# Two transformer layers on one core: another order of the opening, two key spans at the layer boundary, and exchanged places for the opening's partial sums

## The chip, the core and the metric

The kernel runs on one core of a Trainium2 chip. The core has TensorE (PE, matrix multiply), VectorE (DVE), ScalarE (ACT), GpSimd (POOL) and SyncE (SP), which issues the DMAs. Each engine takes its own instructions in the order in which the program lists them, and waits where one needs the result of another engine. The metric is the device time of one execution in microseconds.

## The reference, cut to what matters

Two layers, each of attention and a feed-forward block, over S = 2048 rows of D = 448 columns, with 16 heads of 28 columns. Both layers use the same weights.

```python
def _A_ref(x, wqkv, wo):
    qkv = (x @ wqkv).reshape(B, S, 3, H, Dh).transpose(2, 0, 3, 1, 4)
    q, k, v = qkv[0], qkv[1], qkv[2]
    p = softmax(einsum("bhqd,bhkd->bhqk", q, k) * Dh ** -0.5)
    return einsum("bhqk,bhkd->bhqd", p, v).transpose(0, 2, 1, 3).reshape(B, S, D) @ wo
def _B_ref(x, w1, b1, w2, b2):
    h = maximum(x @ w1 + b1, 0)
    return (h * h) @ w2 + b2
for _ in range(2):
    x = x + _A_ref(layernorm(x), wqkv, wo)
    x = x + _B_ref(layernorm(x), w1, b1, w2, b2)
```

The hidden width F is 1792. Inputs and outputs are bf16. Softmax needs 16 heads x 2048 x 2048 exponentials in each layer.

## The kernel before, in words

**Scores and exponentials.** Heads are taken four at a time (a group g of four; G = 4 groups), each head in 32 rows of its own, so that four small matmuls run side by side. A *unit* is one head's scores of 256 queries against 256 keys (or 128 queries against 512 keys): 512 columns of 128 partitions, one PSUM bank. There are 2048 units, 1024 in each layer. Up to three units make one score group in a PSUM tile `sc` (line 809), and one exponential on ScalarE (line 834) turns them into bf16 weights `pt`. Two such tiles are in turn.

VectorE takes some of the third units of a group off ScalarE and computes their exponential with five operations (lines 890, 904, 910, 916 and 923): the first reads the scores from PSUM, the others build the power of two and a polynomial. Its scratch is `v_i`, `v_e`, and where possible a second set in a part of the K tile of the other layer that is not in use. `apart` decides which unit goes there: none in the last `STOP` units; none when the load of VectorE over the past 14 us is above `BUSY`, or above `LOW` if the feed-forward work is behind a line that `LINES` draws (first unit, last unit, number of blocks); and when fewer than `LAG` units are left in the current pass, it takes one of the next pass, whose keys must be there.

**Passes.** A *pass* is one query block, one group g and one span of keys. Its products with V (line 983) add up in one PSUM bank. When a pass does not cover all keys, its sum is copied aside by VectorE (line 1006), and later passes of the same block and group add to it (line 1008). `part` names the place of such a partial sum: it lies in the K tile of the other layer, 256 columns of float32 for each block, from the end of the tile backwards. In layer 0 that tile's last 512 bf16 columns are also VectorE's second scratch set, for query blocks 2 to 6.

The order of the passes is a list. In layer 0 `OPENING` gives (block, first key tile, last key tile) for query blocks 0 and 1, since keys come in while scores already run; the other blocks take all 16 key tiles at once. At the boundary, query blocks 0 to 2 of layer 1 start on the keys that are already made while the last blocks of layer 0 still pass through projection and feed-forward: `CUTS` splits the key tiles into spans, and within a span all three blocks and four groups come in turn (lines 662 to 664). The unit numbers follow: layer 1 starts at unit 1024; a span of n key tiles for three blocks and four groups takes 24 n units.

**The rest of a layer.** `first_block` normalises two tiles of 128 rows, transposes them (line 493, evicted on line 505), and `qkv` makes K (evicted on lines 573 and 575), Q (569 and 571) and V (601 and 603). `early` blocks (the first two) may use ScalarE for evictions, up to score group 8, and the banks of the score tiles. `chain` does the rest for a query block: output projection with the sum to x (line 1114), layer norm (line 448), hidden layer (1161 and 1168), second product, and in layer 0 the Q, K and V of layer 1.

**What sets the order.** Each of these is a stream of operations with a priority (a small number goes first) and an estimated duration. A planner picks, step by step, the operation that can start first, and writes the instructions in that order; it holds lower work on TensorE back if it would make the next scores late. So a change of a priority or a threshold moves instructions everywhere after it. Priorities: scores 0, exponentials 1, products with V 2, VectorE's first step 1.5, evictions 3.5, `chain` 4 and up, a VectorE unit's other steps `V_PRIO`, and 3.6 (`V_LATE`) once `V_WAIT` us have passed, and 1.8 once the unit is `V_AGE` groups old or its pass is `V_PAST` units past.

Of the kernel before, what the change touches and what calls it, by code (L numbers as in the profile page):

```python
# [18 lines left out]
G = 4  # L19
QB = 512  # L20
QR = 256
# [14 lines left out]
DCLK = 0.2  # L36
OWN = 2
HALF = 320
LINES = ((280, 1312, 8.0), (1440, 2040, 7.0))
MARGIN = 2.0  # L40
LOW = 0.6
TURNS = 1
ENDU = 100
HOTE = 0.8
WSTOP = ('wk', 0)
XT = 1
VEND = 1
OPENING = ((0, 0, 2), (0, 2, 4), (1, 0, 4), (0, 4, 8), (1, 4, 8), (0, 8, 12), (0, 12, 16), (1, 8, 16))
ONE = 1
GATE = [None, None, ('Q', 0, 0, 0), ('Q', 0, 0, 0), ('s', 8), ('s', 8), ('s', 8), ('s', 8)]  # L50
EARLY = 2
# [1 line left out]
SLACK = 0.5  # L53
WINDOW = 2.8
C_PRIO = 1.5
V_PRIO = 6.0
V_LATE = 3.6
V_LAST = 1.8
V_AGE = 7
V_PAST = 2  # L60
OWN3 = 0
FIRST = 90
V_FIRST = 9.2
V_WAIT = 4.5
NEAR = 9
FAR = 15
KEEP = 4
LAG = 6
LEAD = 20
LAST = 690  # L70
BUSY = 0.95
SPAN = 14.0
NPT = 11
NOS = 3
# [11 lines left out]
THIRD = 1  # L86
NL = 0
NLP = 3.8
STOP = 90
HSTOP = 0  # L90
CHUNK = 2
EV = 3.5
CUTS = (0, 8, 12, 16)


class Res:
# [121 lines left out]
def kernel(  # L218
# [13 lines left out]
    _, S, D = A_x.shape  # L232
# [28 lines left out]
    pl = Planner()  # L261
# [13 lines left out]
    wv = const.tile([P, NDC, D], DT.bfloat16, name="wv")  # L275
# [12 lines left out]

    def part(l, qb, g):
        keys = K_sb[1 - l][:, g, :].bitcast(DT.float32)  # L290
        return keys[:, S // 2 - (qb + 1) * QR:S // 2 - qb * QR]

    st_qk = V_sb[1][:, :, :, :].rearrange("p t h r -> p (t h r)")[:, 0:NDC * 2 * D]
    st_qk = st_qk.rearrange("p (c n) -> p c n", c=NDC)
# [240 lines left out]
    def mm_tile(subs, evac, ev_dur, deps, any_engine=False, sets=(), early=False, post=(), acq=None, alone=0):  # L535


        box = {}
        mms = [(c0, n, lhsT, rhs, i == 0, i == len(ops) - 1, own)
               for c0, n, ops in subs for i, (lhsT, rhs, *own) in enumerate(ops)]  # L540
        first = last = None
        i = 0
        while i < len(mms):
            dur, k = 0.003, i
            while k < len(mms) and (k == i or dur + mms[k][1] / 2400 < (0.6 if i == 0 and alone else 0.46) and not (alone and k == alone)):
                dur += max(0.07, mms[k][1] / 2400 + 0.003)
                k += 1

            def fn(e, part=mms[i:k], i=i):
                if i == 0:  # L550
                    box["t"] = bank(first, "mt")
                for c0, n, lhsT, rhs, a, b, _ in part:
                    nc.tensor.matmul(box["t"][:, c0:c0 + n], lhsT=lhsT() if callable(lhsT) else lhsT, rhs=rhs,  # L553
                                     start=a, stop=b)
            own = list({d for m in mms[i:k] for d in m[6]})
            last = Op("PE", dur, fn, deps=(list(deps) if i == 0 else [last]) + own,
                      acq=None if i else pools_now(early) if early else spare(len(mms)))
            first = first or last
            yield last
            i = k  # L560
        e = Op(engs_now(early) if any_engine else ("DVE",), ev_dur, lambda e: evac(e, box["t"]), deps=[last], rel=first, acq=acq, sets=sets)
        pl.spawn(EV, iter([e, *[p(e) for p in post]]))
        return e
# [14 lines left out]
    def qkv(l, t0, nt, xnT, own_xt, ends, early=False):  # L578
        n, q0 = nt * P, t0 * P
        r = QB // n  # L580
        last = None

        def turned(w, dst, key, wkey, g0, r=r):
            nonlocal last
            d = dst[:, g0, q0:q0 + n] if r == 1 else dst[:, g0:g0 + r, q0:q0 + n]
            last = yield from mm_tile(
                [(i * n, n, [(w[:, dc, 4 * g:4 * g + 4, :], xnT[:, dc, 0:n]) for dc in range(NDC)])
                 for i, g in enumerate(range(g0, g0 + r))],
                copy_to(d, q_scale if key == "Q" else None), 0.14 + 0.00109 * r * n, [*ends, *[(wkey, g) for g in range(g0, g0 + r)]], True,
                [(key, l, g, tb) for g in range(g0, g0 + r) for tb in range(t0, t0 + nt)], early and (t0 or g0 == 0))  # L590

        def values():
            nonlocal last
            for tb in range(t0, t0 + nt):
                if l == 1:
                    yield Op("POOL", 0.2, lambda e, tb=tb: nc.gpsimd.memset(V_sb[1][:, tb, :, DH:DHP], 1.0))
                def evv(e, t, tb=tb):
                    o = V_sb[l][:, tb, :, 0:DH]
                    i = t[:, 0:D].rearrange("p (h r) -> p h r", r=DH)
                    if e == "ACT":  # L600
                        nc.scalar.copy(out=o, in_=i)
                    else:
                        nc.vector.tensor_copy(out=o, in_=i)
                j = tb - t0
                last = yield from mm_tile(
                    [(0, D, [(xnT[:, dc, j * P:(j + 1) * P], wv[:, dc, :]) for dc in range(NDC)])],
                    evv, 0.62, [*ends, ("wv",), *([("s", 1)] if early else [])], True, ("V", l, tb), early)

        gs = [(0, 1), (1, 1), (2, 2)] if early and ONE else [(g, r) for g in range(0, G, r)]
        ks = [(wk, K_sb[l], "K", "wk", *g) for g in gs]  # L610
        qs = [(wq, Q_sb, "Q", "wq", *g) for g in gs]
        if l == 0 and t0 == 0:
            yield from turned(*ks[0])
            yield from turned(*qs[0])
            for a, b in zip(ks[1:-1], qs[1:-1]):
                yield from turned(*a)
                yield from turned(*b)
            if not VEND:
                yield from values()
            for a, b in zip(ks[-1:], qs[-1:]):  # L620
                yield from turned(*a)
                yield from turned(*b)
            if VEND:
                yield from values()
            yield Op("DVE", 0.0, None, deps=[last], rel=own_xt)
        else:
            for a in ks[:-1]:
                yield from turned(*a)
            yield from values()
            yield from turned(*ks[-1])  # L630

            def queries():
                if l == 0 and t0 >= 4:
                    yield Op("-", 0.0, None, deps=[("V", 0, tb) for tb in range(NTB)])
                for a in qs:
                    yield from turned(*a)
                yield Op("DVE", 0.0, None, deps=[last], rel=own_xt if own_xt.res else None)
            if l == 0:
                pl.spawn(8 + 0.1 * t0, queries())
            else:  # L640
                yield from queries()

    def first_block(blk):
        early = blk < EARLY
        gate = [] if GATE[blk] is None else [GATE[blk]]
        xnT, own_xt, ends = yield from layernorm(2 * blk, 2, lambda j: [("x", blk // 2, blk % 2), *gate, *([("xT", TILES)] if blk == 1 and XT else [])], early,
                                            place=K_sb[1][:, :, (blk - 2) * QR:(blk - 1) * QR] if 2 <= blk <= 5 else None)
        yield from qkv(0, 2 * blk, 2, xnT, own_xt, ends, early)
# [8 lines left out]

    for qb, lo, hi in OPENING:
        add_passes(0, [qb], (lo, hi))
    for qb in range(2, len(blocks[0])):  # L660
        add_passes(0, [qb], [0, 16])
    for cut in zip(CUTS, CUTS[1:]):
        for qb, gs in enumerate(AHEAD):
            add_passes(1, [qb], cut, gs)
        if cut[1] == CUTS[-2]:
            bridged = len(passes)
    for qb in range(len(blocks[1])):
        gs = AHEAD[qb] if qb < len(AHEAD) else range(0)
        add_passes(1, [qb], [0, 16], [g for g in range(G) if g not in gs])
    units = []  # L670
    for pi, (l, qb, g, kbs, first, last) in enumerate(passes):
        r = 4 // blocks[l][qb][1]
# [15 lines left out]
    def behind(i):  # L688

        l = 0 if i < LINES[0][1] else 1  # L690
        a, b, n = LINES[l]
        return done[l] < (min(i, b) - a) / (b - a) * n * per[l] - MARGIN
# [10 lines left out]
    def apart(i, now, us, soon=SOON):  # L703

        if len(units) - i < STOP or not LEAD <= len(gbuf) <= LAST:
            return None
# [3 lines left out]
        j = i  # L710
        if i + LAG > ends_at[units[i][0]]:
            j = ends_at[units[i][0]] + 1
# [11 lines left out]
        if any(pl.tok.get(d) is None or pl.tok[d].end + LAT["DVE"] > now for d in needs(units[j])):  # L724
            return None
        if pl.load(SPAN, "DVE") > (LOW if behind(i) else BUSY):
            return None
# [151 lines left out]
    def a_unit(gi, x, src, unit, l):  # L879
# [15 lines left out]
        yield c  # L895
        pl.spawn(lambda now: V_LAST if e_now[1] - gi >= V_AGE or at[0] > ends_at[unit[0]] + V_PAST else V_LATE if now > c.end + V_WAIT else V_PRIO if gi > FIRST else V_FIRST, a_rest(gi, c, box, unit))

# [35 lines left out]
    def p_stream():  # L933


        for pi, (l, qb, g, kbs, first, last) in enumerate(passes):
# [18 lines left out]
            while todo:  # L955
                now = [kb for kb in todo if done(kb)][:some]
                if len(now) < min(some, len(todo)):
                    kb = next(kb for kb in todo if not done(kb))
                    if ("u", pi, kb) not in pl.tok or any(k < 3 and ("e", gi) not in pl.tok for gi, k, _ in where[pi, kb]):
                        yield from got(kb)  # L960
                        continue
                    if (e_now[1] - min(gi for gi, _, _ in where[pi, kb]) < NPT - KEEP and e_now[1] < len(gbuf) - 1
                            and len(todo) > len(now) + 1):
# [271 lines left out]
    pl.spawn(9.6, warm_up())  # L1235
    pl.spawn(9, late_setup())
    for b in range(NTB // 2):
        pl.spawn(4 + 0.5 * b, first_block(b))
    pl.run()


# [28 lines left out]
```

The softmax here doesn't subtract the row's maximum and nothing guards it: scores larger than these inputs give would overflow.

## Time and profile before

| | |
|---|---|
| time, median of 3 | 888.03 us (887.72 to 888.74) |
| span of the profiled execution | 884.1 us |
| TensorE, VectorE, ScalarE busy | 824.2, 786.8, 868.4 us |
| granted clock of TensorE | 1.000 |
| exponentials of three units, of two units, on ScalarE | 532, 151 |
| units on VectorE | 150 |

The stretches of the run, from the windows of the trace:

| us | what | ScalarE busy | VectorE busy |
|---|---|---|---|
| 0 to 19.7 | opening | 16.13 | 14.86 |
| 19.7 to 131.5 | first query blocks of layer 0 | 111.34 of 111.84 | 100.73 |
| 131.5 to 441.1 | layer 0 | 309.60 of 309.60 | 285.38 |
| 441.1 to 520.3 | first span of layer 1 | 79.20 of 79.20 | 74.38 |
| 520.3 to 560.2 | second span | 39.90 of 39.90 | 32.72 |
| 560.2 to 612.5 | third span | 51.65 of 52.30 | 47.41 |
| 612.5 to 822.3 | layer 1 | 209.80 of 209.80 | 196.44 |
| 822.3 to 867.9 | last exponentials | 45.60 of 45.60 | 27.05 |
| 867.9 to 884.1 | tail | 5.18 of 16.20 | 7.83 |

A line of the profile names the source line, the engine, the operation, what it writes and reads, how often it came, then busy time and mean duration, and behind the last bar the idle time of its engine before it and what ended that. The durations of instructions that follow one another overlap in part, so the distance of two starts is what counts for an engine that never waits.

### The profile page before, as it was taken

How to read it: one execution, taken by the hardware profiler on the slowest of the kernel's cores; microseconds unless marked ns; L12 is line 12 of the kernel's file. 1: busy time of each engine (PE TensorE's matmuls, PEld its weight loads, DVE VectorE, ACT ScalarE, POOL GpSimd, SP SyncE). 2: the span in 40 equal slices, each digit the busy share in tenths (PEclk: the TensorE clock that was granted, in tenths of full speed). 3: DMA queues.
4: the chain of work that ended last, by engine and by line, in shares of the span. 5: the costliest groups of instructions: out<-in, count | busy, mean ns of one | idle time of the engine just before them, and what ended most of it. 6: DMA issues, size and time to landing. Idle time of an engine off the chain costs nothing.

```text
span 884.1 us, 28887 instructions
## 1 busy us (share of the span) xinstructions
PE 824.2 (93%) x12707; PEld 453.5 (51%) x12707; DVE 786.8 (89%) x1561; ACT 868.4 (98%) x706; POOL 39.1 (4%) x98
## 2 busy tenths in 40 slices
PE   8999989999999999999989999888999999999998
PEld 4555544544545545454454554445454554545566
DVE  7988898999899999998799999898999999899754
ACT  8999999999999999999999999999999999999995
POOL 3100000001000000000101000000000000000000
PEclk9999999999999999999999999999999999999999
DMA  9100000000000000000000000011000000000100
GB/s 261 43 3 2 24 19 14 14 15 15 15 2 15 14 14 15 14 3 14 1 3 2 1 2 2 3 39 40 20 8 25 15 25 25 15 14 14 32 14 18
DMA packets 33914, 18.42 MB, mean 21 GB/s; under 512 B 18874, under 2 KB 33339, under 8 KB 33788
## 3 DMA queue, kind: packets, MB, share of 16 engines
q1 hardware_dynamic: 33788, 16.58, 6.7%
q8 instruction: 99, 1.62, 0.8%
q14 instruction: 27, 0.22, 0.1%
HBM read 14.26 MB, written 2.07 MB: 18 GB/s over the span
## 4 chain that ended last, share of the span: by engine, by line
ACT 71%; PE 11%; issue 11%; DVE 4%; DMA 2%; SPq 1%; POOL 0%; DVEq 0%; ACTq 0%
ACT pt L834 71%; PE mt L553 4%; PE sc L809 3%; PE oT L983 2%; DMA dn<-oT_sb 1%; PE sc L553 1%; DMA scr<-dn 1%; DVE st L448 1%; DMA rec<-scr 0%; SPq L303 0%; DMA x_sb<-in_A_x_dram 0%; PE mt L1219 0%; DVE V_sb L923 0%; DVE r L1161 0%; DVE v_i L890 0%
## 5 line engine op out<-in xcount | busy, mean ns | idle before, releaser
L834 ACT ACTIVATE pt<-sc 128x1536 bf16<-128x1536 f32 (+1 forms) x683 | 854.2, 1565 | 2.6 <-PE sc L809 2.6
L809 PE MATMUL sc<-Q_sb,K_sb 32*128 32x256 bf16 (+1 forms) x5732 | 320.3, 265 | 47.8 <-ACT pt L834 41.8
L809 PEld LDWEIGHTS <-K_sb 32*128 32x128 bf16 x5732 | 152.4, 92 | 226.2 <-issue 194.3
L983 PE MATMUL oT<-pt,V_sb 128*32 128x256 bf16 (+1 forms) x4046 | 152.3, 268 | 0.9 <-ACT pt L834 0.4
L553 PE MATMUL mt<-xnT,w 128*128 128x256 bf16 (+1 forms) x928 | 120.1, 269 | 2.4 <-DVE xnT L505 1.3
L983 PEld LDWEIGHTS <-V_sb 128*32 128x32 bf16 x4352 | 92.1, 96 | 46.6 <-issue 43.8
L553 PEld LDWEIGHTS <-w 128*128 128x128 bf16 x952 | 78.5, 98 | 36.4 <-issue 26.8
L1161 DVE TENSOR_SCALAR r<-mt 128x512 bf16<-128x512 f32 (+1 forms) x107 | 72.7, 680 | 11.2 <-PE mt L553 10.8
L553 PE MATMUL mt<-w,V_sb 128*128 128x448 bf16 (+2 forms) x288 | 68.3, 346 | 0.0
L890 DVE TENSOR_SCALAR v_i<-sc 128x512 int32<-128x512 f32 x85 | 58.1, 684 | 4.1 <-PE sc L809 3.4
L916 DVE SCALAR_TENSOR_TENSOR v_i<-v_i 128x512 f32<-128x512 uint16 x85 | 58.3, 686 | 1.5
L910 DVE SCALAR_TENSOR_TENSOR v_e<-v_i,v_e 128x512 f32<-128x512 uint16 x85 | 58.2, 685 | 0.8
L890 DVE TENSOR_SCALAR K_sb<-sc 128x512 int32<-128x512 f32 x65 | 44.4, 684 | 13.4 <-PE sc L809 13.3
L1114 DVE TENSOR_TENSOR x_sb<-x_sb,mt 128x448 bf16<-128x448 bf16 (+2 forms) x63 | 38.0, 603 | 11.2 <-PE mt L553 11.1
L916 DVE SCALAR_TENSOR_TENSOR K_sb<-K_sb 128x512 f32<-128x512 uint16 x65 | 44.5, 685 | 1.3 <-PE mt L553 0.2
L910 DVE SCALAR_TENSOR_TENSOR K_sb<-K_sb 128x512 f32<-128x512 uint16 x65 | 44.4, 684 | 1.0 <-PE mt L553 0.7
L470 POOL TENSOR_TENSOR ve<-mv,eps_t 128x2 f32<-128x2 f32 (+1 forms) x34 | 8.0, 235 | 831.3 <-DVE mv L449 831.3
L1219 PE MATMUL mt<-xn,ident 128*128 128x448 bf16 x124 | 42.5, 357 | 1.5 <-DVE oT_sb L1008 0.8
L448 DVE BATCH_NORM_STATS2 st<-x_sb 128x6 f32<-128x448 bf16 x64 | 39.4, 615 | 1.7 <-DMA x_sb<-in_A_x_dram 1.2
L553 PEld LDWEIGHTS <-V_sb 128*128 128x128 bf16 x302 | 24.9, 98 | 25.1 <-issue 11.2
L923 DVE SCALAR_TENSOR_TENSOR V_sb<-v_i,v_e 128x512 bf16<-128x512 f32 x54 | 36.8, 682 | 0.2
L904 DVE TENSOR_SCALAR v_e<-v_i 128x512 int32<-128x512 int16 x85 | 35.6, 418 | 0.3
(107 smaller groups left out, 784.1 us busy)
## 6 DMA issues: line engine op xcount, KB each, us to landing
rec<-scr SPq DMA_DIRECT2D x56, 128.0 KB
x_sb<-in_A_x_dram SPq DMA_DIRECT2D x8, 224.0 KB
out_dram<-x_sb SPq DMA_DIRECT2D x15, 112.0 KB
w<-in_B_w_dram SPq DMA_DIRECT2D x1, 1568.0 KB
w<-in_B_w_dram SPq DMA_DIRECT2D x1, 1344.0 KB
dn<-oT_sb SPq DMA_DIRECT2D x56, 4.0 KB
V_sb<-in_A_wqkv_dram SPq DMA_DIRECT2D x4, 168.0 KB
scr<-dn SPq DMA_DIRECT2D x28, 8.0 KB
```

Source lines behind the costliest of these rows:

```text
L448: nc.vector.bn_stats(out=st[:, :], in_=x_sb[:, t0 + j, :])
L553: nc.tensor.matmul(box["t"][:, c0:c0 + n], lhsT=lhsT() if callable(lhsT) else lhsT, rhs=rhs, start=a, stop=b)
L809: nc.tensor.matmul(dst[k][:, i * nt * P:(i + 1) * nt * P], lhsT=K_sb[l][rows, g, (kb + i) * P:(kb + i + 1) * P], rhs=Q_sb[rows, g, t0 * P: ...
L834: t = nc.scalar.activation(out=pt[:, 0:n], in_=gbuf[gi]["sc"][:, 0:n], func=AF.Exp, scale=float(np.log(2.0)) * 2.0 ** -FRAC)
L890: t = nc.vector.tensor_scalar(out=box["i"], in0=two(src), scalar1=EXP_BIAS, scalar2=EXP_LOW, op0=ALU.add, op1=ALU.max)
L910: nc.vector.scalar_tensor_tensor(out=flt("e"), in0=box["f"], scalar=root, in1=flt("e"), op0=ALU.add, op1=ALU.mult)
L916: nc.vector.scalar_tensor_tensor(out=flt("i"), in0=box["f"], scalar=lin, in1=box["f"], op0=ALU.add, op1=ALU.mult)
L923: nc.vector.scalar_tensor_tensor(out=box["two"](pd), in0=flt("i"), scalar=low, in1=flt("e"), op0=ALU.add, op1=ALU.mult)
L983: nc.tensor.matmul(box["t"][DHP * hh:DHP * hh + DHP, 0:n], lhsT=V_sb[l][:, kb + i, 4 * g + hh, :], rhs=p[:, c0:c0 + n], start=begin and kb ...
L1114: nc.vector.tensor_tensor(out=x_sb[:, tb, lo:hi], in0=x_sb[:, tb, lo:hi], in1=t[:, 0:hi - lo], op=ALU.add)
L1161: nc.vector.tensor_scalar(out=r[:, 0:w], in0=t[:, 0:w], scalar1=0.0, scalar2=None, op0=ALU.max)
L1219: nc.tensor.matmul(t[:, 0:D], lhsT=ident[:, :], rhs=xns[0][:, 0:D], start=True, stop=True)
```

## The change

The change reorders the opening: V of the first two row blocks now waits until scores are on their way (score group 4 for the first block, 6 for the second), the second block's K is made in two pieces of two groups each, K stands ahead of V in all blocks but the first, the second block's V and Q become streams of their own, and later row blocks start at other priorities. The last two passes of `OPENING` change places, and so do the partial sums of its two blocks in `part`, so that those of the block that ends last stay clear of VectorE's second scratch set. At the layer boundary the keys are split in two spans (tiles 0 to 9 and 10 to 15) where there were three (0 to 7, 8 to 11, 12 to 15). Thresholds of the planner that decide how many units VectorE takes, and when their steps go first, are set anew to fit. The arithmetic of the result is the same; partial sums are added in other pieces.

```diff
-LINES = ((280, 1312, 8.0), (1440, 2040, 7.0))
+LINES = ((280, 1312, 7.8), (1440, 2040, 6.6))
-LOW = 0.6
+LOW = 0.8
-OPENING = ((0, 0, 2), (0, 2, 4), (1, 0, 4), (0, 4, 8), (1, 4, 8), (0, 8, 12), (0, 12, 16), (1, 8, 16))
+OPENING = ((0, 0, 2), (0, 2, 4), (1, 0, 4), (0, 4, 8), (1, 4, 8), (0, 8, 12), (1, 8, 16), (0, 12, 16))
-V_PRIO = 6.0
+V_PRIO = 7.0
-V_AGE = 7
-V_PAST = 2
+V_AGE = 8
+V_PAST = 3
-V_WAIT = 4.5
+V_WAIT = 5.0
-KEEP = 4
-LAG = 6
+KEEP = 5
+LAG = 8
-BUSY = 0.95
+BUSY = 0.97
-STOP = 90
+STOP = 100
-CUTS = (0, 8, 12, 16)
+CUTS = (0, 10, 16)
...
     def part(l, qb, g):
         keys = K_sb[1 - l][:, g, :].bitcast(DT.float32)
-        return keys[:, S // 2 - (qb + 1) * QR:S // 2 - qb * QR]
+        b = int(qb == OPENING[-1][0]) if l == 0 else qb
+        return keys[:, S // 2 - (b + 1) * QR:S // 2 - b * QR]
...
-                    evv, 0.62, [*ends, ("wv",), *([("s", 1)] if early else [])], True, ("V", l, tb), early)
-
-        gs = [(0, 1), (1, 1), (2, 2)] if early and ONE else [(g, r) for g in range(0, G, r)]
+                    evv, 0.62, [*ends, ("wv",), *([("s", 4 if tb < 2 else 6)] if early else [])], True, ("V", l, tb), early)
+
+        gs = ([[0, 1], [1, 1], [2, 2]] if t0 == 0 else [[0, 2], [2, 2]]) if early else [(g, r) for g in range(0, G, r)]
...
             for a in ks[:-1]:
                 yield from turned(*a)
-            yield from values()
             yield from turned(*ks[-1])
+            if l == 0 and t0 == 2:
+                pl.spawn(6.0, values())
+            else:
+                yield from values()
...
-                pl.spawn(8 + 0.1 * t0, queries())
+                pl.spawn(3.9 if t0 < 4 else 8 + 0.1 * t0, queries())
...
-        pl.spawn(4 + 0.5 * b, first_block(b))
+        pl.spawn((4, 4.5, 5, 5.5, 6.5, 6.5, 7.5, 7.5)[b], first_block(b))
```

## The prediction

> **What bounds the kernel now.** I read the page's table of engines and its chain first, then the groups of instructions by shape, then the timeline of ScalarE in the opening, and last the layer boundary.
>
> ```profile
> PE 824.2 (93%) x12707; PEld 453.5 (51%) x12707; DVE 786.8 (89%) x1561; ACT 868.4 (98%) x706; POOL 39.1 (4%) x98
> ...
> ACT 71%; PE 11%; issue 11%; DVE 4%; DMA 2%; SPq 1%; POOL 0%; DVEq 0%; ACTq 0%
> ```
>
> ScalarE (ACT) is busy for 98% of the span and is 71% of the chain that ends last. The groups by shape say with what:
>
> ```profile
> L834 ACT ACTIVATE pt<-sc 128x1536 bf16<-128x1536 f32 x532 | 750.5, 1658 | 1.8 <-PE sc L809 1.8
> L834 ACT ACTIVATE pt<-sc 128x1024 bf16<-128x1024 f32 x151 | 174.9, 1236 | 0.9 <-PE sc L809 0.9
> L890 DVE TENSOR_SCALAR v_i<-sc 128x512 int32<-128x512 f32 x85 | 58.1, 684 | 4.1 <-PE sc L809 3.4
> L890 DVE TENSOR_SCALAR K_sb<-sc 128x512 int32<-128x512 f32 x65 | 44.4, 684 | 13.4 <-PE sc L809 13.3
> ```
>
> A unit is 512 score columns. 532 x 3 + 151 x 2 = 1898 units are exponentiated on ScalarE and 85 + 65 = 150 on VectorE (DVE): 2048 in all. The mean durations overlap; from start to start the trace has 1.330 us for three units and 0.903 us for two, so a unit moved to VectorE takes 0.427 us off ScalarE. 532 x 1.330 + 151 x 0.903 = 844 us. The first exponential starts at 9.37 and the last ends at 867.9 us; the tail of 16.2 us after it is feed-forward work. So the time is an opening of some 14 us, 844 us of exponentials, a few microseconds of gaps, and the tail. Only three things can move it: gaps in the opening, the number of VectorE units, and a stall of ScalarE somewhere.
>
> The opening on ScalarE (start, duration):
>
> ```profile
> 9.37 1.45 ACT L834 ACTIVATE pt<-sc 128x1536 bf16<-128x1536 f32 x1 [0.49 <-PE sc L809]
> 11.63 1.45 ACT L834 ACTIVATE pt<-sc 128x1536 bf16<-128x1536 f32 x1 [0.82 <-PE sc L809]
> 13.36 0.53 ACT L601 CAST V_sb<-sc 128x448 bf16<-128x448 f32 x1 [0.28 <-PE sc L553]
> 14.12 0.53 ACT L601 CAST V_sb<-mt 128x448 bf16<-128x448 f32 x1 [0.23 <-PE mt L553]
> 14.54 4.14 ACT L834 ACTIVATE pt<-sc 128x1536 bf16<-128x1536 f32 x3
> 18.95 0.53 ACT L601 CAST V_sb<-mt 128x448 bf16<-128x448 f32 x1 [0.26 <-PE mt L553]
> 19.66 41.38 ACT L834 ACTIVATE pt<-sc 128x1536 bf16<-128x1536 f32 x32 [0.18 <-PE sc L809]
> ```
>
> From 9.37 to 19.66 us there are five exponentials (6.65 us), so 3.64 us are lost: 0.93 before the second, 1.58 before the third, 1.13 before the sixth. Three copies of V stand in the last two gaps.
>
> The boundary: instructions that touch K from 530 to 565 us (duration min/median/max, then first and last start).
>
> ```profile
> L1008 DVE TENSOR_TENSOR K_sb<-oT,K_sb x11: 414/417/425, 530.9 to 564.6; 128x256 f32<-128x256 f32 x11
> ...
> L575 DVE CAST K_sb<-mt x2: 685/689/693, 547.0 to 552.2; 128x512 bf16<-128x512 f32 x2
> ```
>
> The last two keys tiles of layer 1 (L575) arrive at 547.0 and 552.2. Counting units along the exponentials, the third span (keys 12 to 15, from unit 1312) starts at 560.2 us. There is slack of 13 us for the first of them.
>
> **What the Trainium skill says.** "Perfetto Trace Analysis", section Identifying the Most-Contended Engine, takes occupancy as a fair measure for ScalarE: the 98% agree with what the gaps show. Its section Optimizing Scalar/DVE Operations says that a profiled duration holds a write-acknowledgement half that overlaps the next instruction; the trace agrees (1658 ns recorded against 1330 between starts; on VectorE 684 against 0.60 us). "ScalarE: Activation LUTs", section What ACT_TABLE_LOAD costs, gives 0.833 ns per element: 512 elements are 427 ns, exactly the step measured here.
>
> **The change part by part.**
>
> *Opening.* V of the first block now waits for score groups 4 (line 607), of the second for group 6, and the second block's K is taken in two pieces of 512 instead of 256, 256, 512, ahead of V. Once exponentials are queued on ScalarE, the copies of V fall to VectorE, which has room (14.9 of 19.7 us). The third group needs the last Q, which VectorE evicts from 12.92 to 13.58 us; an exponential followed such an eviction by 0.50 us in the first group (8.87 to 9.37), so it can start at 14.08: 0.46 gained. The sixth group needs K of the second block; its normalised rows are ready at 11.65 us, but TensorE transposes them only at 14.55, behind V. With V out of the way the 1.13 us gap should close. The gap before the second group depends on lines that stay. Sum 0.46 + 1.13 = **1.6 us** off; the bounds are 0 (the transposes still wait for a PSUM bank) and 3.64 (all gaps gone).
>
> *Two spans at the boundary* (CUTS 0, 8, 12, 16 to 0, 10, 16). Three query blocks x four groups, 12 in all, now add a partial sum once instead of twice. That takes away 12 adds of line 1008, 0.34 us apart from the next instruction: 4.1 us of VectorE. A VectorE unit is four operations at 0.60 and one at 0.34, 2.74 us; so 1.5 more units fit. Passes of 8 units also become 12. A VectorE unit is put off to the next pass if fewer than LAG units are left, and then needs that pass's keys; from 543.6 to 559.2 us none starts, and VectorE is busy for 12.2 of the 17 us from 543 to 560. I take one unit more from there. Sum +2.5 units.
>
> *The price of it.* Keys 10 to 15 are now needed from unit 1264, not 12 to 15 from unit 1312. Unit 1264 runs at 540.1 us, and the pass asks for key tile 14 eight units later, at 542.7; scores run some 2 us ahead of exponentials, so K must stand at about 540.5, and it stands at 547.7 now (547.0 + 0.69). That is 7 us late. Against it: seven adds before 547 are gone (2.4 us), a VectorE unit yields to the chain for longer (V_WAIT 4.5 to 5.0, V_AGE 7 to 8, V_PAST 2 to 3), and 20-unit passes hold the second PSUM bank for a smaller share of the time. If scores stop for lack of K, everything behind them on ScalarE stops, but VectorE then does little except the chain. Bounds 0 and 7 us; I take **0.7 us**, since the last stretch of that chain (adds to x at 532.3 and 538.3, K at 547.0) is made of instructions waiting among VectorE units that the planner can order otherwise.
>
> *Thresholds.* BUSY 0.95 to 0.97 lets VectorE take a unit at a load 2% higher: over the 570 us outside opening, boundary and end at most 11 us, four units; I take two, as its load is above the old mark only part of the time (the windows show 0.92 and 0.94). Lower LINES with LOW at 0.8 release at most 0.4 blocks of layer-1 work to the end, where VectorE has 18.6 us idle of 45.6 from 822 to 868: +1.5 units. STOP 100 takes units away from the last ten places, at one unit in twelve: -1. V_PRIO 7 hardly matters: only second-half opening streams have priorities near. Sum +2.5 units; bounds -5 and +12.
>
> The exchanged partial sums (the `part` function) cost nothing: the same copy in another 256 columns, as the block that finishes last keeps clear of VectorE's second scratch set. The order of the last two passes of the opening only moves which block's chain starts first (unit 224 instead of 192); VectorE idles 10% there, which hides it.
>
> Sum: +5 units x 0.427 = 2.1 us off, 1.6 off, 0.7 on: 888.0 - 3.0 = **885.0 us**.
>
> **The rivals.** (a) *The deadline bites.* Two spans cost ScalarE a stall of 5 to 8 us at some 540 us, and the opening gives 1.6: 888.0 - 1.6 - 1.1 + 6.5 = 891.8, slower. For it: the 7 us lateness, and lower LINES, which push the chain less. Against: VectorE is freed by the stall itself. (b) *VectorE gets no more units* since it is already at 92 to 94%, and the earlier work in the opening only shifts a wait: about -0.8 us, 887.2. For it: TensorE at 93% lets chain work in only between scores. (c) *Both work fully*: 12 units (5.1 us) and 2.5 us in the opening, no stall: 880.4. For it: 24 us of idle VectorE between 131 and 441 us. Against: most of it is in pieces shorter than one operation.
>
> **How the numbers follow.** Forecast 0.48, (a) 0.21, (b) 0.17, (c) 0.14. Faster by over 0.2% is under 886.25: nearly all of the forecast and (c), 0.62 and a little of (b), 0.63; within 0.2% (to 889.8) 0.16; slower 0.21. The range runs from 880.5, about the middle of (c), to 890.0, the lower edge of (a); its unknowns are the stall (0 to 7) and the units (-3 to +14, 7 us).
>
> **What would show it.** Right: the sixth exponential near 18 us with V copied on line 603; 155 instructions of line 890 and as many fewer whole triples on line 834; 36 adds on line 1008 for 48; the last L575 before 545. Wrong: a gap on ScalarE before 560 us released by scores, which wait for L575; or fewer than 150 units; or a tail above 16.2 us since more feed-forward work is left over.

## The result, and the profile after

The changed kernel takes 883.52 us (median of 4, 882.43 to 884.26) against 887.88 us for the kernel before in the same series: ratio 0.9951, 95% interval 0.9933 to 0.9968, or 4.4 us off. The forecast was 885.0 us. Executions of one kernel differ in how long TensorE ran at half clock. The two profiles, both at a mean granted clock of 1.000, are of executions of 885.87 and 882.89 us, and in the three later series the kernel before took 885.5 to 885.8 us (medians) at that clock. So at equal clock the change is worth about 3 us; the rest of the 4.4 is probably half clock in the kernel before, whose clock in this series is not on record.

Line numbers move by one to four in the changed file: the exponential is line 838 (834 before), the first step of a VectorE unit 894 (890), K is evicted on line 576 (575). The page's engines and chain, after:

```profile
PE 823.4 (93%) x12678; PEld 449.4 (51%) x12678; DVE 795.6 (90%) x1570; ACT 865.0 (98%) x703; POOL 40.8 (5%) x98
...
ACT 70%; issue 11%; PE 11%; DVE 7%; DMA 0%; SPq 0%; POOL 0%; ACTq 0%
```

The same engine bounds it, ScalarE, with 3.4 us less to do, while VectorE does 9 us more. The groups by shape give the units:

```profile
L838 ACT ACTIVATE pt<-sc 128x1536 bf16<-128x1536 f32 x528 | 748.2, 1648 | 2.5 <-PE sc L813 2.1 <-PE oT L987 0.4
L838 ACT ACTIVATE pt<-sc 128x1024 bf16<-128x1024 f32 x155 | 181.3, 1238 | 0.1
L894 DVE TENSOR_SCALAR v_i<-sc 128x512 int32<-128x512 f32 x87 | 59.6, 685 | 8.1 <-PE sc L813 7.7
L894 DVE TENSOR_SCALAR K_sb<-sc 128x512 int32<-128x512 f32 x67 | 45.8, 684 | 10.1 <-PE sc L813 9.8
```

87 + 67 = 154 units are on VectorE, four more than before. At 0.427 us each that is 1.7 us. The opening on ScalarE:

```profile
10.46 1.45 ACT L838 ACTIVATE pt<-sc 128x1536 bf16<-128x1536 f32 x1 [0.49 <-PE sc L813]
12.36 1.45 ACT L838 ACTIVATE pt<-sc 128x1536 bf16<-128x1536 f32 x1 [0.44 <-PE sc L813]
14.77 13.54 ACT L838 ACTIVATE pt<-sc 128x1536 bf16<-128x1536 f32 x10 [0.96 <-PE sc L813]
28.66 31.98 ACT L838 ACTIVATE pt<-sc 128x1536 bf16<-128x1536 f32 x25 [0.35 <-PE oT L987]
```

In this execution the projection weights came in 1.1 us later, so everything is read from the first exponential on. From the third exponential on there is no gap until 28.3 us, and no copy of V on ScalarE. The sixth exponential starts 8.3 us after the first; before it was 10.3. That is 2.0 us: 0.50 ahead of the third, 1.13 ahead of the sixth, and 0.36 ahead of the second. The last is not shown to be the opening's work: the time lost ahead of the second exponential lies between 0.4 and 1.5 us in the traces with the new opening, and between 0.5 and 1.3 in those with the old.

The boundary, instructions that touch K from 530 to 565 us:

```profile
L1012 DVE TENSOR_TENSOR oT_sb<-oT,K_sb x4: 418/422/425, 549.1 to 560.4; 128x256 f32<-128x256 f32 x4
...
L576 DVE CAST K_sb<-mt x2: 681/682/684, 538.3 to 543.0; 128x512 bf16<-128x512 f32 x2
```

The adds into K (the middle span) are gone, and the last keys stand at 538.3 and 543.0, nearly 9 us earlier than before. Unit 1272, the first that needs them, runs at 540.7, and ScalarE has no gap there. The tail after the last exponential is 16.3 us (16.2 before).

From the first exponential to the end of the profile it is 874.7 us before and 870.7 after, 4.1 less: 2.0 in the opening, 1.7 from units, 0.4 from small gaps (one of 1.0 us at 607 us, for one, is gone). The later start, 1.1 us, takes the spans' difference down to 3.0.

### The profile page after: what moved, and what is told of

It is laid out like the page before. It is cut to its first block, busy times and chain, and to the rows that moved or that the text cites. A ratio compares the mean times of both kernels' runs of the same rounds, so it can differ in the third digit from the quotient of the medians.

```text
span 881.1 us, 28830 instructions
## 1 busy us (share of the span) xinstructions
PE 823.4 (93%) x12678; PEld 449.4 (51%) x12678; DVE 795.6 (90%) x1570; ACT 865.0 (98%) x703; POOL 40.8 (5%) x98
## 4 chain that ended last, share of the span: by engine, by line
ACT 70%; issue 11%; PE 11%; DVE 7%; DMA 0%; SPq 0%; POOL 0%; ACTq 0%
ACT pt L838 70%; PE mt L554 5%; PE sc L813 3%; PE oT L987 2%; DVE st L449 1%; PE sc L554 1%; DVE r L1165 0%; DMA x_sb<-in_A_x_dram 0%; SPq L304 0%; DVE v_e L914 0%; DVE K_sb L894 0%; DVE mv L450 0%; DVE K_sb L576 0%; DVE v_i L894 0%; DVE K_sb L914 0%
## 5 line engine op out<-in xcount | busy, mean ns | idle before, releaser
L813 PEld LDWEIGHTS <-K_sb 32*128 32x128 bf16 x5708 | 150.2, 92 | 226.1 <-issue 192.0
L894 DVE TENSOR_SCALAR K_sb<-sc 128x512 int32<-128x512 f32 x67 | 45.8, 684 | 10.1 <-PE sc L813 9.8
L920 DVE SCALAR_TENSOR_TENSOR K_sb<-K_sb 128x512 f32<-128x512 uint16 x67 | 45.9, 686 | 1.1
L914 DVE SCALAR_TENSOR_TENSOR K_sb<-K_sb 128x512 f32<-128x512 uint16 x67 | 45.7, 682 | 0.4
L1223 PE MATMUL mt<-xn,ident 128*128 128x448 bf16 x119 | 40.5, 358 | 0.3 <-DVE xn L521 0.2
L554 PEld LDWEIGHTS <-V_sb 128*128 128x128 bf16 x302 | 24.8, 98 | 24.4 <-issue 10.6
```

The source lines that it names most:

```text
L813: nc.tensor.matmul(dst[k][:, i * nt * P:(i + 1) * nt * P], lhsT=K_sb[l][rows, g, (kb + i) * P:(kb + i + 1) * P], rhs=Q_sb[rows, g, t0 * P: ...
L894: t = nc.vector.tensor_scalar(out=box["i"], in0=two(src), scalar1=EXP_BIAS, scalar2=EXP_LOW, op0=ALU.add, op1=ALU.max)
L914: nc.vector.scalar_tensor_tensor(out=flt("e"), in0=box["f"], scalar=root, in1=flt("e"), op0=ALU.add, op1=ALU.mult)
L920: nc.vector.scalar_tensor_tensor(out=flt("i"), in0=box["f"], scalar=lin, in1=box["f"], op0=ALU.add, op1=ALU.mult)
L1223: nc.tensor.matmul(t[:, 0:D], lhsT=ident[:, :], rhs=xns[0][:, 0:D], start=True, stop=True)
```

## The experiments

Three parts can be taken singly: the *opening* (order of passes, exchanged places, V behind score groups, K in pieces and ahead of V, priorities of the first blocks), the *spans* (CUTS) and the *thresholds* (LINES, LOW, V_PRIO, V_AGE, V_PAST, V_WAIT, KEEP, LAG, BUSY, STOP). Each ratio is to the kernel before in the same series. The number of units is that of the program; the rest is read from the traces (us), one execution of each kernel: start of the sixth exponential after the first; start of the last two K evictions of layer 1; most time lost between two exponentials from 535 to 560; time after the last exponential. "Changed, three spans" is also the opening and the thresholds together, so that all eight subsets of the three parts are there.

| kernel | ratio (95% interval) | units | 6th exp. | last K | gap | tail |
|---|---|---|---|---|---|---|
| before | 1 | 150 | 10.3 | 547.0, 552.2 | under 0.2 | 16.2 |
| changed | 0.9951 (0.9933 to 0.9968) | 154 | 8.3 | 538.3, 543.0 | under 0.2 | 16.3 |
| opening alone | 1.0112 (1.0080 to 1.0144) | 140 | 8.1 | 559.3, 560.7 | under 0.2 | 24.3 |
| spans alone | 1.0027 (1.0019 to 1.0036) | 153 | 10.1 | 546.5, 549.6 | 4.6 | 16.2 |
| thresholds alone | 1.0068 (1.0046 to 1.0090) | 150 | 9.9 | 537.3, 542.2 | under 0.2 | 24.3 |
| opening and spans | 1.0077 (1.0050 to 1.0104) | 145 | 8.5 | 549.4, 551.0 | 6.5 | 16.2 |
| spans and thresholds | 0.9981 (0.9971 to 0.9991) | 152 | 10.6 | 539.2, 544.6 | under 0.2 | 17.6 |
| changed, three spans | 0.9976 (0.9966 to 0.9987) | 152 | 8.7 | 542.7, 546.1 | under 0.2 | 16.1 |
| thresholds, HOTE 0.9 | 1.0056 (1.0041 to 1.0071) | 150 | 9.9 | 537.3, 542.3 | under 0.2 | 23.2 |
| changed, V behind group 1 | 0.9958 (0.9943 to 0.9973) | 154 | 10.4 | 539.4, 544.1 | under 0.2 | 16.2 |
| changed, old ages | 1.0084 (1.0069 to 1.0099) | 154 | 8.3 | 551.8, 553.5 | 12.2 | 16.0 |
| changed, old lines | 0.9971 (0.9960 to 0.9982) | 153 | 8.3 | 537.8, 539.0 | under 0.2 | 16.3 |
| changed, old places | 0.9966 (0.9953 to 0.9979) | 154 | 8.3 | 537.8, 542.5 | under 0.2 | 16.3 |
| changed, old pass order | 0.9965 (0.9952 to 0.9977) | 155 | 9.2 | 538.6, 543.3 | 0.3 | 17.7 |

**The parts alone.**

> The kernel before with the opening edits alone (order of passes and exchanged partial sums, V waiting for score groups, K in two pieces and ahead of V, priorities of the first blocks); three spans and the old thresholds stay. Its program has 140 units on VectorE where the kernel before has 150. Theory (sum of ScalarE): the opening gives 2.0 us back and ten units cost 10 x 0.427 = 4.3 us: 887.9 - 2.0 + 4.3 = 890.2 us, slower than before. Rival (the gain of the change is the opening, units are of no weight): 885.9 us.

```diff
 # before, with the opening's edits
-OPENING = (..., (0, 8, 12), (0, 12, 16), (1, 8, 16))
+OPENING = (..., (0, 8, 12), (1, 8, 16), (0, 12, 16))
...
```

Measured 896.6 us, 11.0 over the kernel before. Both expectations missed. The opening itself gave 2.2 us and the ten units took 4.3; but the tail grew by 8.1 us, two gaps of 1.0 and 0.5 us opened at 842 to 844, and two of 0.6 and 0.8 at 165 to 168; both pairs stand in or just behind a stretch of TensorE at half clock. The profile is of the slowest of its four executions. The tail is read below.

> The kernel before with CUTS = (0, 10, 16) alone. 153 units on VectorE. Theory (sum of ScalarE): 887.9 - 3 x 0.427 = 886.6 us if the keys come in time. Rival (the earlier deadline bites when V stands ahead of the second half of K and the thresholds are the old ones): a gap on ScalarE near 540 us of 3 to 7 us that scores release, 889.6 to 893.6 us. The last K evictions of layer 1 tell which: by 541 us or after.

```diff
-CUTS = (0, 8, 12, 16)
+CUTS = (0, 10, 16)
```

Measured 888.28 us, 2.7 over. The rival held. The waits of this kernel from 535 to 560 us:

```profile
ACT pt L834 <- PE sc L809: 4.3, 1, 4.3
```

One wait of 4.3 us (4.6 us of lost time between exponentials, at 547 us): the scores wait for the keys evicted at 546.5. 4.6 lost less 1.3 for three units is 3.3, near the 2.7 measured.

> The kernel before with the new thresholds alone (LINES, LOW, V_PRIO, V_AGE, V_PAST, V_WAIT, KEEP, LAG, BUSY, STOP). 150 units as before. Theory (sum of ScalarE): 887.9 us, no change within 0.5. Rival of the prediction (the thresholds alone bring some two units): 886.9 us. If the keys of layer 1 come earlier than 547.0 us here, the thresholds are what moved them to 538 in the changed kernel.

```diff
 # before, with the ten thresholds of the change
-LOW = 0.6
+LOW = 0.8
...
-BUSY = 0.95
+BUSY = 0.97
```

Measured 892.45 us, 6.9 over: both missed on the time, and the last sentence held. The keys come at 537.3 with no other edit, so it is the thresholds that move them. The loss is again a tail of 24.3 us, and it does not hang on the clock alone: the one execution with a granted clock of 1.000 took 890.56 us, still 5.0 us more than the kernel before at that clock.

> The changed kernel with the old thresholds: opening edits and two spans. 145 units on VectorE. Theory (sum of ScalarE): 887.9 - 2.0 + 5 x 0.427 = 888.0 us with no stall. Rival (without the new thresholds the keys come late at the boundary): a stall of 3 to 7 us on top, 891 to 895 us.

```diff
 # before, with the opening's edits and
-CUTS = (0, 8, 12, 16)
+CUTS = (0, 10, 16)
```

Measured 892.86 us, 7.3 over. The rival held: the keys at 549.4, a gap of 6.5 us.

**Do thresholds make two spans possible?**

> The kernel before with two spans and the new thresholds, the opening as before. 152 units on VectorE. Theory (the thresholds bring the keys of layer 1 to 537 to 543 us, as they did alone, and that is what makes two spans possible): no gap over 1 us near 547 us, the keys by 543, 2 units less on ScalarE: 0.9 us faster than the kernel before if the end keeps TensorE's full clock; 8 to 10 us slower if the end loses it (half clock for 3.4 and 6.8 us, as in the runs with thresholds or opening alone). Rival (the opening edits, with K ahead of V, bring the keys in time): a stall of 4 to 7 us near 547 us.

```diff
 # before, with the ten thresholds of the change and
-CUTS = (0, 8, 12, 16)
+CUTS = (0, 10, 16)
```

Measured 885.33 us, 1.4 under the kernel before. The theory held: keys at 539.2 and 544.6, no gap. The end lost the clock once, for 3.4 us at 865, with a tail of 17.6 us. To the changed kernel's 4.4 us it lacks 3.0. Two units (0.9), the end (1.3) and the opening (10.6 against 8.3) would make 4.5, where the traces differ by 3.8 from the first exponential on and the medians by 3.0: the opening's gain does not all reach the end.

> The changed kernel with V_AGE 7, V_PAST 2, V_WAIT 4.5 and KEEP 4 put back: the priorities of VectorE's units against the feed-forward chain, and what products with V wait for, as before. 154 units, as many as in the changed kernel. Theory (a VectorE unit that yields longer to the chain is what brought the keys of layer 1 from 547 to 538 us): the keys come after 543 us, ScalarE stalls 3 to 7 us near 545 us, and the time is 880.5 + 5 us on the scale of the changed kernel's 881 us span, about the kernel before's or slower. Rival (it is LINES and LOW, or LAG, that decide): keys by 540 us, no stall, the changed kernel's time within 0.7 us.

```diff
 # the changed kernel, with
-V_AGE = 8
-V_PAST = 3
-V_WAIT = 5.0
-KEEP = 5
+V_AGE = 7
+V_PAST = 2
+V_WAIT = 4.5
+KEEP = 4
```

Measured 893.71 us, 7.8 over the kernel before, with as many units as the changed kernel. ScalarE near the boundary:

```profile
535.03 7.13 ACT L838 ACTIVATE pt<-sc 128x1024 bf16<-128x1024 f32 x6
554.01 7.31 ACT L838 ACTIVATE pt<-sc 128x1024 bf16<-128x1024 f32 x6 [11.85 <-PE sc L813]
```

and VectorE there:

```profile
551.75 0.69 DVE L576 CAST K_sb<-mt 128x512 bf16<-128x512 f32 x1 [1.96 <-PE mt L554]
```

ScalarE stands idle for 11.85 us until scores that need these keys. The stall is longer than either expectation. With the scores stopped TensorE stops too, and its clock halves for 6.8 us; but that lengthens the last steps to the keys by little more than 1 us (the eight transposes take 1.04 us against 0.62 in the changed kernel, 16 products for K 3.57 against 1.05 for eight). Most of the delay stands in VectorE's steps before that: the last two adds to x ahead of the keys start at 539.4 and 544.5 us, with steps of VectorE units between them, against 522.1 and 529.6 in the changed kernel. The theory holds: with the rest of the change in place, these four thresholds bring the keys 13.5 us earlier. Which of the four does it was not run.

> The changed kernel with LINES = ((280, 1312, 8.0), (1440, 2040, 7.0)) and LOW = 0.6 put back. 153 units, one fewer. Theory (the age thresholds decide on the keys; LINES only give a unit or two): keys by 541 us, no stall over 1 us, 0.4 us slower than the changed kernel. Rival (the lines decide): another time of the keys by more than 3 us.

```diff
 # the changed kernel, with
-LINES = ((280, 1312, 7.8), (1440, 2040, 6.6))
-LOW = 0.8
+LINES = ((280, 1312, 8.0), (1440, 2040, 7.0))
+LOW = 0.6
```

Measured 883.21 us, ratio 0.9971 against 0.9951 for the changed kernel; the intervals overlap. Keys at 537.8, 153 units. The lines don't decide on the keys.

> The changed kernel with CUTS = (0, 8, 12, 16) put back. 152 units on VectorE, two fewer than the changed kernel, and 12 adds more. Theory (two spans are worth their units): 0.9 us slower than the changed kernel, so 3.5 us faster than the kernel before; or, if the end loses the clock, 5 to 6 us slower than before. Rival (two spans are worth more, since the short passes of the middle span leave VectorE idle and the wait on the keys shifts): a further gap of 1 us or more between 540 and 615 us.

```diff
 # the changed kernel, with
-CUTS = (0, 10, 16)
+CUTS = (0, 8, 12, 16)
```

Measured 884.73 us, 2.0 under the kernel before; expected were 3.5. The rival's gap comes as two short ones (0.66 and 0.41 us at 575 and 595), and there is a half clock from 822 to 829 us with 2.9 us of small gaps, which nobody foresaw. By the ratios two spans are worth some 2.2 us here (0.9976 - 0.9951), but the intervals just touch, and clocks are in it: the four executions at a granted clock of 1.000 took 883.2 to 884.6 us, the changed kernel's two 882.4 and 882.9. At equal clock it is some 1.2 us, of which units are 0.9.

**The opening's own gain.**

> The changed kernel with V of the first two blocks waiting for score group 1 again, as before. 154 units. Theory of the prediction (the opening's gain is V out of the way of scores and off ScalarE): three copies of V return to ScalarE, the sixth exponential starts 9.5 to 10.3 us after the first instead of 8.3, and the time is 1.2 to 2.0 us above the changed kernel. Rival (the gain is K of the second block in two pieces ahead of V): 8.3 to 8.8 us, under 0.5 us above the changed kernel.

```diff
 # the changed kernel, with
-*([("s", 4 if tb < 2 else 6)] if early else [])
+*([("s", 1)] if early else [])
```

Measured 883.02 us, ratio 0.9958. ScalarE again:

```profile
11.88 1.45 ACT L838 ACTIVATE pt<-sc 128x1536 bf16<-128x1536 f32 x1 [0.79 <-PE sc L813]
13.61 0.53 ACT L602 CAST V_sb<-sc 128x448 bf16<-128x448 f32 x1 [0.28 <-PE sc L554]
14.37 0.53 ACT L602 CAST V_sb<-mt 128x448 bf16<-128x448 f32 x1 [0.23 <-PE mt L554]
14.79 4.14 ACT L838 ACTIVATE pt<-sc 128x1536 bf16<-128x1536 f32 x3
19.26 0.59 ACT L574 CAST K_sb<-sc 128x512 bf16<-128x512 f32 x1 [0.33 <-PE sc L554]
20.03 25.42 ACT L838 ACTIVATE pt<-sc 128x1536 bf16<-128x1536 f32 x19 [0.19 <-PE sc L813]
```

The sixth exponential is 10.4 us after the first, 2.1 later than in the changed kernel. Of these, 1.7 us are the gaps ahead of the third and the sixth, with two copies of V and one of K back on ScalarE; the rest is the gap ahead of the second. So V's wait is the whole of the gain that can be put down to the opening, as the prediction had it. But the time is only 0.6 us above the changed kernel by the ratios, within their intervals (1.3 us from the first exponential to the end of the traces). Part of it is given back: the changed kernel has a gap of 0.5 us at 28.7 us and 0.6 us at 825 us that this one has not.

**The exchange and the order of passes.**

> The changed kernel with the partial sums of the opening's two blocks in their old places. Its instructions are the same, in the same order, with 154 units; only the addresses of the partial sums differ. Theory of the prediction (the exchange keeps the block that ends last clear of VectorE's second scratch set, which units of block 2 write from 125 us on): the first writes into that scratch wait for the last adds of block 0, a wait of up to a few microseconds on VectorE near 125 us, 0 to 2 us on the time. Rival (the adds are over before any unit of block 2 takes the second set): no difference, within 0.3 us of the changed kernel.

```diff
 # the changed kernel, with
-        b = int(qb == OPENING[-1][0]) if l == 0 else qb
+        b = qb
```

This kernel changes part of the computation: block 0's partial sums lie where VectorE's second scratch set is, and are overwritten before they are added. VectorE in it:

```profile
117.40 0.69 DVE L894 TENSOR_SCALAR K_sb<-sc 128x512 int32<-128x512 f32 x1
118.13 0.43 DVE L908 TENSOR_SCALAR K_sb<-K_sb 128x512 int32<-128x512 int16 x1
...
119.80 0.41 DVE L1012 TENSOR_TENSOR oT_sb<-oT,K_sb 128x256 f32<-128x256 f32 x1
...
122.97 0.42 DVE L1012 TENSOR_TENSOR oT_sb<-oT,K_sb 128x256 f32<-128x256 f32 x1
```

The scratch is written at 117.4 and 118.1; the last two adds of block 0 read it at 119.8 and 123.0. The theory of a wait was wrong: nothing waits. The time is that of the changed kernel (883.39 us, 0.9966, the intervals overlap). The exchange shows no cost, but is not optional once block 0 ends last.

> The changed kernel with the last two passes of OPENING in their old order, so that block 0 ends at unit 192 and its chain starts 32 units earlier; part then gives the old places. 155 units, one more than the changed kernel. Theory (sum of ScalarE): 0.4 us faster than the changed kernel, if the keys come by 541 us and the end keeps the clock. Rival (the order was changed for the gaps at 106 and 108 us, where the first chain's Q, K and denominators met the scores): these gaps of 0.5 and 0.4 us come back and the time is 0.5 us above the changed kernel.

```diff
 # the changed kernel, with
-OPENING = (..., (0, 8, 12), (1, 8, 16), (0, 12, 16))
+OPENING = (..., (0, 8, 12), (0, 12, 16), (1, 8, 16))
```

Measured 882.78 us, 0.9965. Neither held clearly: a gap of 0.8 us at 84 us, none at 106; 155 units; the clock halves at 864.6 and the tail is 17.7 us, but this profile is of the slowest of six executions, and the other five had a granted clock of 1.000 (882.07 to 883.08 us). No kernel tried is clearly ahead of the changed one, and what the order of passes, the lines or the exchange add by themselves is below what these runs can tell.

**The tail.**

> The kernel before with the new thresholds and HOTE = 0.9 for 0.8: in the last 100 units the planner repeats score matmuls up to a load of 0.9 of TensorE where it stopped at 0.8. 150 units, as with the thresholds alone. Theory (a stretch of some 3.4 us with TensorE under 60% busy halves its clock for the next 3.4 us, and that puts the last feed-forward work off behind the last exponential): the clock stays full near 838 us, the tail is 16 us and not 24, and the time is that of the kernel before within 1 us, 7 us under the thresholds alone. Rival (the thresholds leave more feed-forward work to the end, whatever the clock): the tail stays at 24 us and the time 6 to 7 us above the kernel before.

```diff
 # before, with the ten thresholds of the change and
-HOTE = 0.8
+HOTE = 0.9
```

Measured 891.85 us, 5.1 over. The rival held. The gaps near 838 us are gone, and the tail is still 23.2 us. So that clock drop is not its cause, as the execution of the thresholds alone at the full clock says too. TensorE in the tail of the kernel with the opening alone (last exponential ends at 871.8),

```profile
871.80 0.35 PE L554 MATMUL sc<-wo,oTn 128*128 128x448 bf16 x1
...
873.30 0.73 PE L554 MATMUL mt<-wo,oTn 128*128 128x448 bf16 x3
875.45 0.36 PE L554 MATMUL mt<-wo,oTn 128*128 128x448 bf16 x1 [1.42 <-DVE oTn L1063]
876.84 0.61 PE L494 MATMUL tp<-ident,xn 128*128 128x128 bf16 x4 [1.03 <-DVE xn L521]
877.96 2.29 PE L554 MATMUL sc<-xnT,w 128*128 128x128 bf16 x20 [0.52 <-DVE xnT L506]
```

and of the changed kernel (last exponential ends at 864.8):

```profile
857.62 0.93 PE L554 MATMUL mt<-wo,oTn 128*128 128x448 bf16 x4
...
864.23 0.74 PE L554 MATMUL sc<-wo,oTn 128*128 128x448 bf16 x3
865.25 0.84 PE L554 MATMUL mt<-xnT,w 128*128 128x128 bf16 x12
```

With the opening alone the output projections (wo) of the last two blocks run one after the other from the end of the last exponential, and TensorE waits for the divided attention sums (oTn) and the layer norm (xn); in the changed kernel, as in the kernel before, the first of them runs 7.2 us ahead of that end, and the first product with w1 starts 0.5 us after it, not 6.1. With it goes the second product of the block ahead: it starts some 15 us before the end of the last exponential in the three kernels with a long tail, 18.5 to 19 in the others. 3.6 us late there go with 7 to 8 us at the end; that the one makes the other is read from the order, not tried. Both forms come out of the planner's order; which of the edits tips it was not isolated.

## Why the prediction was right

The forecast was 3.0 us; it came to about 3 at equal clock and 4.4 between the medians. The sum came near, but partly by luck: the units and the stall are wrong in what they were made of.

**Opening: right, mechanism and size.** 1.6 us were forecast, 2.0 measured. Its terms: 0.46 ahead of the third exponential, measured 0.50 (1.58 to 1.08); the 1.13 us ahead of the sixth closed. That is 1.63. The 0.93 ahead of the second, which I took as fixed, went to 0.57; as that gap varies by more than this between the traces, it is luck. The transposes moved from 14.55 to 13.13 us. The run with V behind group 1 shows that V is the cause in the opening; it also shows that less than this reaches the end (0.6 us by the ratios, within their intervals).

**Units: right in sum (5 forecast, 4 came), wrong in the terms.** Spans: +2.5 forecast, +3 in the run alone. Thresholds: +2.5 forecast; alone they give 0, on top of the other two edits 9 (145 to 154). Opening: I gave it no term, and only for the order of its last two passes a reason ("VectorE idles 10% there, which hides it"); alone it loses 10, and in the changed kernel the order by itself costs one (155 to 154). A planner's parts do not add up, and a sum of single terms was the wrong form. LINES and LOW at +1.5 are shown at +1 (154 against 153), and the age thresholds with KEEP at 0; BUSY, STOP, LAG and V_PRIO were not run singly. That +5 came near +4 is luck.

**The deadline: the mechanism was right, its size not.** That K "stands 7 us late" for two spans was read correctly from the trace: with spans alone ScalarE loses 4.6 us, with opening and spans 6.5. The prediction named V_WAIT, V_AGE and V_PAST as what would help, and kept 0.7 us of stall. The run with the old ages shows that they (with KEEP) decide it, 12.2 us or none. The seven adds fewer, which it put at 2.4 us, moved the first of the keys by 0.5 with spans alone (547.0 to 546.5). Keys at 538.3 left nothing of the 0.7.

**Rival (a), the deadline, was real for both kernels with two spans and the old thresholds.** Every part alone is slower than the kernel before, and so are the opening and the spans together. The thresholds with either of the other parts gain 1.4 and 2.0 us, all three 4.4.

**Not seen at all: the end.** I left the tail at 16.2 us, and only in the last sentence named a longer one. It stayed at 16.3, but three of the kernels tried have 23 to 24 us there; nothing in the prediction told which it would be, so that it held is luck.

**The sum of the time.** 13 us to the end of the opening's gaps, 844 of exponentials and 16.2 of tail are 873 of the 884.1 us, so the "few microseconds of gaps" are about 11. Most of them are hundredths of a microsecond at each exponential, 10.2 us behind the sixth before and 9.8 after, and don't bear on the difference.

## What to carry to other kernels

Where one engine is busy from end to end, count what it must do and look for stalls; everything else acts through these two, up to its last instruction; then comes the tail, which has to be read for itself. Where a planner writes the order, price a change of several parts as a whole, and look for cliffs first: a date by which a result must stand (the keys at 540 us) and the last block's place before or after the last of the bound engine's work cost 5 to 12 us here, and ten units 4. Before a difference of a few microseconds is put down to a change, compare executions with the same granted clock. When passes are reordered, ask again which scratch shares memory with what is still to be read.

## What the runs showed of the hardware

TensorE's granted clock fell to half for stretches of 3.41 or 6.83 us. The windows of the kernel with the opening alone (length, TensorE busy, then granted clock):

```profile
832.40:835.80 3.40, 3.40 (x96) 1.00 0.12 34
835.80:839.20 3.40, 2.00 (x89) 0.99 0.07 6
839.20:842.60 3.40, 3.40 (x46) 0.50 0.15 39
842.60:846.00 3.40, 3.40 (x114) 1.00 0.02 5
...
873.20:876.60 3.40, 1.19 (x6) 1.00 0.02 5
876.60:880.00 3.40, 2.65 (x24) 0.52 0.00 0
880.00:883.40 3.40, 3.40 (x35) 0.50 0.00 0
883.40:886.80 3.40, 3.40 (x63) 0.98 0.00 0
```

Here 2.00 us busy of 3.40 were followed by one such stretch at half clock, 1.19 of 3.40 by two. The share alone does not decide, though, and the 60% of the expectation above is no rule. Spans and thresholds together, then spans alone:

```profile
861.83:865.24 3.41, 2.27 (x61) 1.00 0.02 5
865.24:868.65 3.41, 3.31 (x42) 0.50 0.00 0
...
543.23:546.64 3.41, 1.87 (x19) 1.00 0.02 5
546.64:550.05 3.41, 3.41 (x45) 1.00 0.00 0
```

2.27 us of 3.41 (67%) were followed by half clock, 1.87 (55%) were not, and in the kernel before 2.61 of 3.40 (863.0 to 866.4 us) were not. In the traces each fall during the work followed a window of 67% or less, but not each such window a fall; busy time here counts modelled ends of matmuls, and what else goes in stays open. The Trainium skill, "TensorE: Matmul & The Clock Gate", Part 1, tells of an activity window of 3.4 us; the length agrees. It matters here because the planner fills TensorE with repeated scores to keep that clock, and a long stall of ScalarE takes the filling away with it: in the 11.85 us stall TensorE did nothing from 543.9 to 547.3 us, and the half clock began there.
